# A weight block's load split by head pairs: one transfer of 128 rows or four of 32

## The chip, the cores and the metric

The kernel runs on one core of a Trainium2 chip. The metric is the device time of one execution in microseconds (us), the median of several. The engines go by their short names: PE is TensorE (matrix products), PEld its weight loads, DVE is VectorE, ACT is ScalarE, POOL is GpSimd, and SP is SyncE, which here issues nearly all DMA transfers. The transfers themselves are carried by the core's 16 DMA engines.

## What is computed

Two layers, one after the other. The first is an mLSTM cell over 4 batches, 8 heads, 768 steps and a head width of 40. The second is a feed-forward layer whose activation is h·cos(h). Between them the heads are laid side by side, so that a row of x holds 8 x 40 = 320 numbers.

```python
# q, k, v, o_gate: (4, 8, 768, 40) float32;  i_gate, f_gate: (4, 8, 768)
for t in range(S):
    m_new = np.maximum(f_gate[:, :, t] + m, i_gate[:, :, t])
    f_stab, i_stab = np.exp(f_gate[:, :, t] + m - m_new), np.exp(i_gate[:, :, t] - m_new)
    m = m_new
    C = f_stab[..., None, None] * C + i_stab[..., None, None] * np.einsum('bhd,bhe->bhde', vt, kt)
    n = f_stab[..., None] * n + i_stab[..., None] * kt
    y[:, :, t] = sigmoid(o_gate[:, :, t]) * (C @ qt) / max(|n . qt|, 1)
x = y.transpose(0, 2, 1, 3).reshape(3072, 320)
h = x @ w_in            # w_in: (320, 2048)
out = (h * np.cos(h)) @ w_out   # w_out: (2048, 320)
```

The two weights reach the device as 64-bit floating-point numbers, because the inputs are made that way. The kernel loads their 32-bit halves and makes float32 of them on the chip.

## The kernel before

The sequence is cut in 6 chunks of 128 steps (`c`), and each chunk has 4 batches (`b`). A pair is a cell, with the number n = 4c + b. The kernel first runs the four cells of chunk 0 (`first_cells`). Then, for every chunk c and every b, it runs `both_parts(c, b)`: a quarter of the feed-forward layer of chunk c, beside the cell (c+1, b) of the next chunk. The instructions of each engine are laid out by hand (a manual schedule) and are carried out in this order.

w_in is loaded in four blocks of 512 columns, `weights_in(0)` to `weights_in(3)`, each used by one b of the first chunk. A row of x is split: the first 32 of every head's 40 numbers go into two operands of 128 rows (four heads each: head 2k+i of pair k goes to operand i), and the remaining 8 of the eight heads into a third of 64 rows. The rows of w_in are brought into the same order by the load. So a block consists of two big pieces and one of leftovers:

```python
WP, WQ = 512, 2 * DM
w_in_bits, w_out_bits = (w.bitcast(I32).rearrange("r (n two) -> r n two", two=2) for w in (moe_w_in, moe_w_out))

def bits_in(n, src, pool, width):
    bits = pool.tile([128, width, 2], I32, name="bits", tag="bits")
    for rows, piece in src:
        nc.sync.dma_start(out=bits[rows, 0:n], in_=piece)
    return bits

def weights_in(f):
    for i in range(NK):                 # NK = 2 big pieces
        src = w_in_bits.rearrange("(k i d) n two -> i k d n two", i=2, d=D)[i, :, 0:DA, ts(f, WP)]
        yield w_in_sb[:, i, ts(f, WP)], bits_in(WP, [(slice(0, 128), src)], pb, WP)
    # ... and the leftovers: two transfers of 64 rows, 8 heads x 8 each
```

Here D = 40 and DA = 32. `src` of a big piece has the dimensions 4 (pairs k), 32 (rows d), 512 columns and 2 words. The pool `pb` has 5 buffers.

A piece that has landed is converted. ACT makes two arrays of its halves, DVE shifts and joins, POOL adds:

```python
def parts(dst, bits):
    ...
    nc.scalar.activation(out=t.bitcast(FP), in_=hi.bitcast(FP), func=AF.Abs)        # L140
    nc.scalar.activation(out=m, in_=lo, func=AF.Copy, scale=2.0 ** -29)             # L142
    return dst, hi, t, m

def join(dst, hi, t, m):
    nc.vector.tensor_scalar(...)            # L146
    nc.vector.tensor_scalar(...)            # L148
    nc.vector.scalar_tensor_tensor(...)     # L150, the last to read the bits
    nc.gpsimd.tensor_tensor(out=dst.bitcast(I32), in0=t, in1=m, op=OP.add)          # L151
```

w_out comes in eight pieces of 640 KB with 128 rows each (`weights_out(p)`, three buffers), which are converted in the same way.

The order of the loads on SP and of the work, cut to what lies around these pieces:

```python
def first_cells():
    ...                         # gates, q, k, v of cells 0 to 2
    load(3)                     # q, k, v of cell 3
    pieces.extend(weights_in(0))
    ...
    load(B)                     # q, k, v of cell 4
    ...
    load_E(B); load_o(1); load_E(B + 1)
    outs.append((0, weights_out(0)))
    ...
    values(2); decay(3); weigh_k(3); state(1); normalize(2); scores(3)
    pg = gates_turn(); warm(1); seam(2); weigh(3)
    join(*parts(*pieces.pop(0)))
    pieces.extend(weights_in(1))
    load(B + 1)
    outs.extend((p, weights_out(p)) for p in range(1, 3))
    seam_out(2); state(2); gates_keep(*pg)
    values(3); normalize(3)
    turn(B)                     # PE turns q and k of cell 4: the first to want them
    join(*parts(*pieces.pop(0)))
    warm(3); seam(3)
    decay_exponents(B)          # DVE, then a mask on POOL; E(4) has to be there
    load_E(B + 2); seam_out(3)
    join(*parts(*pieces.pop(0)))
    state(3); turn_out(B, False); decay(B); weigh_k(B); sigmoid(1)

def both_parts(c, b):
    n = (c + 1) * B + b
    f2 = 2 * b
    up = Up(c, f2)              # PE: x @ w_in, two 128-column blocks (L612, leftovers L615)
    scores(n)
    for e in range(2): up.near(e)      # ACT (L620)
    ...
    for e in range(2): up.rest(e)      # DVE (L623)
    ...
    for e in range(2):
        up.sin(e)                      # ACT (L628)
        up.gate(e)                     # DVE (L632)
    ...
    if begin:                          # c == b == 0
        h = out_parts(); w = parts(*pieces.pop(0))
    elif pieces:
        join(*parts(*pieces.pop(0)))
    ...                                # decay of the next cell (ACT)
    down(c, f2 - 1)                    # PE: @ w_out (L644)
    load(n + 2); values(n); normalize(n); out_join(...); load_E(n + 3)
    ...                                # two more pieces likewise
    up = Up(c, f2 + 1); seam(n); ...; down(c, f2)
    if c == 0 and b + 2 < B:
        pieces.extend(weights_in(b + 2))
    turn(n + 1); ...
```

Of the kernel before, what the change touches and what calls it, by code (L numbers as in the profile page):

```python
# [29 lines left out]
def kernel(  # L30
# [26 lines left out]
    HP = H // 2  # L57
# [9 lines left out]
    DA, DL, T4 = 32, 8, 4  # L67
# [11 lines left out]
    pb = ctx.enter_context(tc.tile_pool(name="pb", bufs=5))  # L79
# [39 lines left out]
    w_in_sb = wp.tile([128, NK, DFF], FP, name="w_in_sb")  # L119
# [5 lines left out]
# [8 lines that stand above are left out]
# [24 lines left out]

    def weights_in(f):
        for i in range(NK):
            src = w_in_bits.rearrange("(k i d) n two -> i k d n two", i=2, d=D)[i, :, 0:DA, ts(f, WP)]  # L160
            yield w_in_sb[:, i, ts(f, WP)], bits_in(WP, [(slice(0, 128), src)], pb, WP)
        src = w_in_bits.rearrange("(h d) n two -> h d n two", d=D)[:, DA:D]

        yield (w_in_l[:, ts(f, 2)].rearrange("p a n -> p (a n)"),
               bits_in(256, [(slice(64 * e, 64 * e + 64), src[:, :, ts(2 * f + e, 256)]) for e in range(2)], pb, WP))
# [492 lines left out]
    def first_cells():  # L658
# [29 lines left out]
        load_o(0, (2, 3))  # L688
        load(3)
        pieces.extend(weights_in(0))  # L690
        wall_in(1, 0, psum_o())
        wall_in(1, 1, psum_o())
# [53 lines left out]
        weigh(3)  # L746
# [4 lines that stand above are left out]
# [35 lines left out]
    def both_parts(c, b):  # L786
# [94 lines left out]
        if c == 0:  # L881
            if b + 2 < B:
                pieces.extend(weights_in(b + 2))
            h = out_parts()
# [45 lines left out]
```

## Time and profile before

| | |
|---|---|
| median of 3 runs | 575.06 us (574.02 to 575.40) |
| span of the profiled execution | 572.1 us |
| PE busy | 547.9 us, 96% |
| DVE, ACT, POOL busy | 350.7, 262.6, 84.7 us |
| moved by DMA | 56.79 MB, 99 GB/s over the span |
| w_in's big transfers | 8 of 512 KB |
| w_in's leftovers | 8 of 128 KB |
| w_out's transfers | 8 of 640 KB |

The page of the profile has the busy time of each engine, then the span cut in 40 equal slices, with a digit for the busy share of each slice in tenths (9 is 90% or more). PEclk is the clock that PE was granted, in the same tenths. The DMA share of a window is the mean busy share of the 16 DMA engines; it can come out above 1 where packets overlap. The chain that ended last is followed back from the last instruction, at each step to what released it. A row of waits reads: engine and instruction that waited, the one it waited for, us in total, how often, the longest. In a row of a window come the window, its length, for each engine its busy us and number of instructions, then PE's clock, the DMA share and GB/s. L612 is a line of the kernel.

### The profile page before, as it was taken

To read this page: it belongs to the slowest core of one execution; us is meant where nothing else is said; L and a number is where in the kernel's file an instruction comes from. 1 tells how busy PE (TensorE), PEld (TensorE's weight loads), DVE (VectorE), ACT (ScalarE), POOL (GpSimd) and SP (SyncE) were. 2 spreads that over 40 slices of the span, in tenths; PEclk is the share of its full clock that TensorE was granted. 3 is DMA by queue.
4 is the path that set the end of the run, shared out by engine and by line. 5 is a ranking of instruction groups with operands and counts; after the bars stand their busy time and mean duration, and the time that the engine had idled before them with its cause. 6 is when DMAs were issued, how large, how long until landed. Compare 5 with 4: busy or idle time off the path is not lost.

```text
span 572.1 us, 8809 instructions
## 1 busy us (share of the span) xinstructions
PE 547.9 (96%) x3247; PEld 326.9 (57%) x3247; DVE 350.7 (61%) x690; ACT 262.6 (46%) x418; POOL 84.7 (15%) x114
## 2 busy tenths in 40 slices
PE   8969894999999999999999999999999999999997
PEld 6855462666566556555565565566555555545554
DVE  5756746675777676676676676676676675313221
ACT  4837728577464255264255264255264341323222
POOL 5522413342311011011011011010000000000000
PEclk9979996999999999999999999999999999999999
DMA  9846695576026564226655026665026200010001
GB/s 140 189 127 181 192 205 155 152 181 144 12 77 135 121 134 103 58 87 135 141 127 127 14 82 131 134 138 131 15 87 144 47 15 1 16 45 1 0 0 46
DMA packets 134026, 56.79 MB, mean 99 GB/s; under 512 B 71600, under 2 KB 130048, under 8 KB 133984
## 3 DMA queue, kind: packets, MB, share of 16 engines
q1 hardware_dynamic: 133840, 56.04, 42.6%
q8 instruction: 25, 0.41, 0.3%
q0 software_dynamic: 96, 0.18, 0.1%
q14 instruction: 17, 0.14, 0.1%
q10 hardware_dynamic: 48, 0.02, 0.0%
HBM read 50.00 MB, written 6.21 MB: 98 GB/s over the span
## 4 chain that ended last, share of the span: by engine, by line
PE 82%; DMA 8%; SPq 4%; DVE 2%; ACT 2%; issue 1%; POOL 1%; ACTq 0%; POOLq 0%
PE po L644 36%; PE pup L612 27%; PE pup L615 8%; DMA bits<-in_moe_w_in_dram 5%; PE hp L482 3%; PE ps L439 3%; DMA qs<-in_q_dram 3%; PE pu L579 2%; SPq L321 2%; PE hp L476 2%; SPq L292 1%; PE pt L420 1%; PE ph L464 1%; POOL w_out_sb L151 1%; ACT wt L140 0%
## 5 line engine op out<-in xcount | busy, mean ns | idle before, releaser
L644 PE MATMUL po<-w_out_sb,g 128*128 128x320 f32 x768 | 220.5, 441 | 4.9 <-POOL w_out_sb L151 4.9
L644 PEld LDWEIGHTS po<-w_out_sb,g 128*128 128x128 f32 x768 | 143.4, 192 | 71.1 <-issue 9.7
L612 PE MATMUL pup<-xT,w_in_sb 128*128 128x512 f32 x384 | 175.0, 598 | 2.0 <-POOL w_in_sb L151 1.7
L620 ACT ACTIVATE n<-pup 128x512 int32<-128x512 f32 x96 | 51.9, 592 | 216.6 <-PE pup L615 216.6
L623 DVE SCALAR_TENSOR_TENSOR n<-pup,n 128x512 f32<-128x512 f32 x96 | 61.8, 685 | 143.6 <-ACT n L620 143.6
L612 PEld LDWEIGHTS pup<-xT,w_in_sb 128*128 128x128 f32 x384 | 71.0, 190 | 78.3 <-issue 67.2
L628 ACT ACTIVATE n<-n 128x512 f32<-128x512 f32 x96 | 58.7, 630 | 11.6 <-DVE n L623 11.6
L365 POOL TENSOR_SCALAR_AFFINE_SELECT E<-E 128x1024 f32<-128x1024 f32 x19 | 20.7, 1091 | 290.5 <-DVE E L364 251.9
L632 DVE SCALAR_TENSOR_TENSOR g<-pup,n 128x512 f32<-128x512 f32 x96 | 61.6, 683 | 1.7
L615 PE MATMUL pup<-xT,w_in_l 64*128 64x512 f32 x192 | 54.2, 641 | 0.3 <-POOL w_in_l L151 0.3
L615 PEld LDWEIGHTS pup<-xT,w_in_l 64*128 64x128 f32 x192 | 14.5, 185 | 36.8 <-issue 34.9
L445 DVE TENSOR_TENSOR E<-ps,E 128x512 f32<-128x512 f32 x48 | 30.6, 679 | 3.4 <-PE ps L439 3.4
L404 DVE STREAM_TRANSPOSE t<-qs 128x512 f32<-128x512 f32 x32 | 32.3, 1088 | 0.0
L373 ACT ACTIVATE E<-E 128x1024 f32<-128x1024 f32 x21 | 22.2, 1057 | 21.5 <-POOL E L365 16.8
L439 PEld LDWEIGHTS ps<-t,t 40*128 40x128 f32 (+1 forms) x384 | 25.0, 188 | 9.7 <-issue 9.2
L439 PE MATMUL ps<-t,t 40*128 40x128 f32 (+1 forms) x384 | 25.8, 274 | 0.0
L364 DVE TENSOR_TENSOR E<-E,tab 128x1024 f32<-128x1024 f32 x19 | 23.1, 1213 | 4.0 <-DMA E<-M_d 4.0
L140 ACT ACTIVATE wt<-bits 128x512 f32<-128x512 f32 (+2 forms) x20 | 13.4, 668 | 26.3 <-DMA bits<-in_moe_w_in_dram 19.8
L373 ACT ACT_TABLE_LOAD x18 | 23.1, 1283 | 0.3
L775 ACT ACT_TABLE_LOAD x18 | 23.1, 1283 | 0.3
L579 PEld LDWEIGHTS pu<-vs,kw 128*104 128x104 f32 x160 | 17.0, 177 | 9.8 <-issue 9.8
L496 DVE STREAM_TRANSPOSE room<-hp 128x128 f32<-128x128 f32 x32 | 8.5, 305 | 22.5 <-PE hp L482 22.5
(130 smaller groups left out, 455.4 us busy)
## 6 DMA issues: line engine op xcount, KB each, us to landing
E<-M_d SPq DMA_DIRECT2D x22, 512.0 KB
bits<-in_moe_w_out_dram SPq DMA_DIRECT2D x8, 640.0 KB
bits<-in_moe_w_in_dram SPq DMA_DIRECT2D x8, 512.0 KB
room<-G_d SPq DMA_DIRECT2D x32, 128.0 KB
ks<-in_k_dram SPq DMA_DIRECT2D x24, 160.0 KB
vs<-in_v_dram SPq DMA_DIRECT2D x24, 160.0 KB
out_dram<-o_sb SPq DMA_DIRECT2D x24, 160.0 KB
qs<-in_q_dram SPq DMA_DIRECT2D x32, 80.0 KB
```

What stands on the lines that cost most here:

```text
L373: nc.scalar.activation(out=Es[n], in_=Es[n], func=AF.Exp, scale=-1.0)
L404: nc.vector.transpose(out=dst.rearrange("r p (t x) -> r p x t", x=T4), in_=src.rearrange("r p (x d) -> r p x d", x=T4)[:, :, :, 0:32])
L439: nc.tensor.matmul(ps[j][:, p], kT[r, p], qT[r, p], start=True, stop=True)
L445: nc.vector.tensor_tensor(out=w, in0=pss[n][j], in1=w, op=OP.mult)
L579: nc.tensor.matmul(pu[0:PR, p].rearrange("p j d -> p (j d)"), pair(kws[n], p)[:, 0:PR], vs[n % NB][:, 2 * p:2 * p + 2].rearrange("p j d -> ...
L612: nc.tensor.matmul(pu, w_in_sb[:, i, ts(block(f2, e), 128)], x(i), start=(i == 0), stop=False)
L615: nc.tensor.matmul(pu, w_in_l[r, f2], x(NK, r), start=False, stop=True)
L620: nc.scalar.activation(out=self.n[e], in_=self.pu[e], func=AF.Copy, bias=0.25)
L623: nc.vector.scalar_tensor_tensor(out=self.n[e].bitcast(FP), in0=self.pu[e], scalar=0.25, in1=self.n[e], op0=OP.add, op1=OP.subtract)
L628: nc.scalar.activation(out=r, in_=r, func=AF.Sin, scale=TWO_PI_DOWN)
L632: nc.vector.scalar_tensor_tensor(out=g, in0=self.pu[e], scalar=TWO_PI, in1=self.n[e].bitcast(FP), op0=OP.mult, op1=OP.mult)
L644: nc.tensor.matmul(po[c][b], gs[c, f][:, ts(b, C)], w_out_sb[:, f], start=(f == 0), stop=(f == NF - 1))
```

## The change

The source of a big piece is no longer handed over as one access pattern of 4 groups of 32 rows. Each head pair gets a transfer of its own: 32 rows of 4096 bytes, into its own 32 partitions of the same buffer. The transfers go out one after the other on SP, where the one stood. What is loaded, where to, and everything after it stay as they are. It is meant to make the loading of w_in's pieces better suited to the DMA engines.

```diff
     def weights_in(f):
         for i in range(NK):
+
             src = w_in_bits.rearrange("(k i d) n two -> i k d n two", i=2, d=D)[i, :, 0:DA, ts(f, WP)]
-            yield w_in_sb[:, i, ts(f, WP)], bits_in(WP, [(slice(0, 128), src)], pb, WP)
+            yield w_in_sb[:, i, ts(f, WP)], bits_in(WP, [(ts(h, DA), src[h]) for h in range(HP)], pb, WP)
         src = w_in_bits.rearrange("(h d) n two -> h d n two", d=D)[:, DA:D]
```

HP is 4, so `h` counts head pairs here. The empty line that is added shifts all later lines of the kernel by one: L612 of the kernel before is L613 of the changed one.

## The prediction

> **What bounds the kernel now.** I read the page first: the busy row and the slices, then the chain that ended last, then the waits of TensorE (PE) and ScalarE (ACT), then windows.
>
> ```profile
> PE 547.9 (96%) x3247; PEld 326.9 (57%) x3247; DVE 350.7 (61%) x690; ACT 262.6 (46%) x418; POOL 84.7 (15%) x114
> PE   8969894999999999999999999999999999999997
> PEclk9979996999999999999999999999999999999999
> PE 82%; DMA 8%; SPq 4%; DVE 2%; ACT 2%; issue 1%; POOL 1%; ACTq 0%; POOLq 0%
> ```
>
> PE is the bound, but not everywhere. A slice is 572.1/40 = 14.3 us; from the eighth on (100 us) PE shows 9 in every slice but the last, at full clock. The holes are in slices 1, 3, 5 and 7, and 3 and 7 have a lower clock too. So whatever is gained is gained before about 104 us, and whatever arrives earlier at 104 us ends earlier at 572, because after it PE has nothing to wait for. The 8% of DMA in the chain are two transfers of w_in of 12.09 and 13.83 us (at 46.02 and 73.90 in the chain by time), and one of q of 15.96 us (at 23.64).
>
> The waits of PE from 20.95 to 104.73 us, then ACT's from 20 to 155 (us in total, times, longest):
>
> ```profile
> PE px L568 <- DVE z L536: 5.8, 1, 5.8
> PE pt L420 <- DMA qs<-in_q_dram: 5.5, 1, 5.5
> PE po L644 <- POOL w_out_sb L151: 4.0, 3, 2.3
> PE pup L612 <- POOL w_in_sb L151: 1.7, 1, 1.7
> ...
> ACT wt L140 <- DMA bits<-in_moe_w_in_dram: 19.8, 4, 11.6
> ```
>
> The first two rows are one story. At 81 us ACT, which works in order, stands 11.64 us at the conversion of a w_in piece (released at 87.81); VectorE (DVE) behind it stands 10.61 us; its z comes late and PE waits 5.8 us. The second: the q of cell 4 was issued at 23.64, right behind w_in's first pieces, and landed at 39.61, while PE was ready at 34.2.
>
> Why are those transfers slow? Windows, with the columns PEclk, DMA share and GB/s at the end. The first lies inside the transfer of the w_in pieces issued at 20.95, the other six are the kernel's stages:
>
> ```profile
> 31.00:39.00 8.00, 3.22 (x30) 2.79 (x28) 3.96 (x11) 3.98 (x10) 1.26 (x1) 0.85 0.24 82
> ...
> 20.95:44.55 23.60, 18.07 (x160) 15.46 (x160) 12.93 (x33) 12.28 (x24) 6.72 (x6) 0.86 0.56 127
> 44.55:66.93 22.38, 20.95 (x107) 12.94 (x107) 16.07 (x31) 19.09 (x29) 7.95 (x9) 1.00 0.59 155
> 66.93:104.73 37.80, 27.09 (x118) 17.24 (x116) 23.49 (x44) 19.02 (x37) 12.08 (x12) 0.86 0.77 198
> 104.73:128.56 23.83, 23.83 (x118) 15.40 (x117) 16.03 (x34) 16.83 (x33) 8.63 (x9) 1.00 0.68 170
> 128.56:152.27 23.71, 22.83 (x108) 14.42 (x108) 16.52 (x30) 16.34 (x28) 6.93 (x7) 1.00 0.44 96
> 152.27:173.70 21.43, 21.43 (x145) 12.49 (x145) 15.62 (x33) 9.81 (x16) 3.63 (x3) 1.00 0.24 66
> ```
>
> In 31 to 39 us the share of 16 engines is 0.24: four busy, twelve idle. The stage of c=0, b=1 lasts 37.80 us; its neighbours, with much the same matmuls, last 23.83 and 23.71.
>
> **What the Trainium skill says.** "DMA: Bandwidth & Descriptors", section on why a DMA increments its semaphore by 16: an HWDGE transfer runs on k engines, the largest k up to 16 that divides the slowest dimension of both access patterns. The source of a big w_in piece is 4 head pairs x 32 rows x columns against 128 partitions: k = 4. The trace agrees: each of these eight transfers has 5 semaphore updates at landing (4 engines, and the sequencer for the rest), the transfers of w_out, q, k, v have 16, and so have the gates' 32-row transfers. The same page, rules for kernel authors, says not to split a transfer over partition halves, because each half already uses all 16 engines; here that premise fails. "TensorE: Matmul & The Clock Gate", Part 1: PE's clock is gated down after idleness and let up again by sustained work. The trace agrees: half clock from 36.7 to 43.5 and from 91.3 to 101.5 us, each after one of the two idles, and nowhere else between 6 us and the end.
>
> **The change, part by part.**
>
> *Adds.* Eight 512 KB transfers become 32 of 128 KB: 24 more issues on SP. The trace's uncontended 16-engine issues take 0.40 (32 gate rows) to 0.57 us, the k=4 ones 0.54 to 0.71. Eight at 0.47 with their gap, less two at 0.67: about +2.4 us of SP for each of the four stages. A piece now has four semaphores to be waited for instead of one; not a tenth of a microsecond. The order of instructions on PE, DVE, ACT and POOL is unchanged.
>
> *Takes away.* Two big pieces now take four engines 64 rows of 4096 B each; at 165 (median) to 210 ns (mean) a row that is 10.6 to 13.4 us, with leftovers and queue 16 to 18 us until the second has landed (20.95 to 37.88; 73.90 to 92.81). With 32 rows over 16 engines it is 2 rows a transfer and engine, 16 for both pieces: 2.6 to 3.4 us. As a check, 640 KB of w_out on 16 engines landed in 4.5 to 6.7 us from issue.
>
> *Moves, step 1 (up to 44.55 us).* w_in's first pieces issue at 20.95 to 24.8, land by about 27, the leftover by 28.5. q of cell 4 issues at 26.1 and lands near 29.5 (1024 rows of 160 B, 64 an engine, 14 to 18 ns each, 1.1 us a transfer), E(4) near 33.5 instead of 44.23. PE goes on at 34.2 instead of 39.74: 5.5 us. The half clock there goes too. Behind it the work of DVE and POOL decides: DVE ends z(3) at 36.4, joins piece 1 until 38.0, subtracts for E(4) until 39.2, the mask on POOL ends 40.4, then ACT runs exp, table load and sigmoid until 44.0, before it evacuates the first up matmul. In the trace that starts at 50.30: about **6.3 us** gained.
>
> *Step 2 (b=0, 22.38 us).* It ends in PE waiting 1.70 us for w_in_sb. ACT's 2.99 us of waiting for a piece at 58.19 goes, so DVE's gate ends 2 us earlier and the joins too: **1.7 us**. At b=1's start PE waits 0.98 us for w_out_sb; that chain moves by about 2.2, so **0.5** more.
>
> *Step 3 (b=1, 37.80 us).* w_in's third block is issued behind w_out's piece 3, which waits for one of three buffers, free at about 54 us; it lands by 64; ACT wants it at 68. The 11.6 us wait goes, and PE's 5.8 and 2.26 us of idle, and the half clock (10.2 us, with some 7 us of matmul in it, 3 to 3.5 us). The stage then is its matmuls: up 4.6 + scores 0.9 + down 4.5 + pq 0.9 + values 1.8 + up 4.6 + seam 1.6 + down 4.5 + turn 0.9 = 24.3, with a first wait of 0.4 to 0.8 left, 25. Of 37.8 less the 2.2 of step 2, 35.6, that is **10.6 us**.
>
> *Step 4 (b=2 on).* PE is busy 23.83 of 23.83; w_in's last block lands about 88 against a need at 93. **0.** At b=3 a wait of 0.88 us for w_out_sb stays.
>
> Sum: 6.3 + 2.2 + 10.6 = 19.1 us. Some of these chains I only followed by hand, and a chain not seen now may end last; I take off 0.6. 575.06 - 18.5 = 556.5.
>
> **Rivals.**
> 1. *SP takes the place.* SP stays in order, only eight transfers are in flight (each waits for the one eight before it), and ten issues stand where four stood. If each took 1 us or more, q, k and E behind them would land late. For it: issues of 3 to 9.7 us stand in the trace. Against: these stand behind the four full engines (the 9.66 us of v at 29.25 ends as w_in lands), so the change removes their cause. It would leave perhaps half: 565.
> 2. *The conversion becomes the bound.* Each piece costs ACT 1.3, DVE 1.6, POOL 1.3 us. In b=1 DVE shows 23.49 us of work, close to the 25 that I give the stage. Against: some 5 us of that are b=0's joins, which lag, and b=2 runs PE without a hole with 16.03. If it holds, step 3 gives 7 instead of 10.6: 560.
> 3. *DMA is full, whatever the engines.* The share is 1.10 in the first 21 us and 0.77 in b=1; squeezing b=1 into 25 us makes it 1.1, if nothing is spread differently. But w_in then is a third of what it was in any one engine, and much of b=1's traffic may lie earlier. If loads then end late, 562.
> 4. *More than I say:* if sigmoid and exp in step 1 overlap better, or the b=3 wait goes too, 554.
>
> **Range and chances.** The two idles of PE with their clocks are the solid part: 5.5 + 5.8 + 2.3 + 1.7 + 3 = 18.3 us without any chain by hand, so even two thirds of it is over 2% (11.5 us). The range of 552.5 to 562 holds rivals 2 to 4. Rival 1 alone puts it at 2% or less. Faster by over 2%: 0.94, within: 0.05, slower: 0.01.
>
> **What would show it.** Right: 16 landings for each w_in transfer; no 0.24 stretch; ACT's wait for w_in bits under 2 us; q's wait of PE gone; full clock from 6 us to the end; b=1 of about 25 us; everything from b=2 on with the same lengths, about 19 us earlier. Wrong: SP issues of w_in over 1 us each with PE waiting for qs or E; or waits for w_out_sb grown to several us in b=1 with DVE full; or a DMA share near 1 from 45 to 85 us with ACT still waiting for bits.

## The result and the profile after

The changed kernel takes 555.10 us (four runs, 555.07 to 555.99) against 574.74 us before (574.02 to 575.40): a ratio of 0.9662, with a 95% interval of 0.9645 to 0.9679. It is 19.6 us faster; 556.5 had been predicted. The span of the profiled execution went from 572.1 to 553.4 us.

DMA's slices on the page of the kernel before:

```profile
DMA  9846695576026564226655026665026200010001
```

The page of the changed kernel (busy row, PE's slices, PE's clock, DMA's slices, the chain by engine):

```profile
PE 542.2 (98%) x3247; PEld 322.9 (58%) x3247; DVE 351.0 (63%) x690; ACT 262.8 (47%) x418; POOL 85.8 (16%) x114
...
PE   8998999999999999999999999999999999999997
...
PEclk9999999999999999999999999999999999999999
DMA  9999969560265751166634065635065000000001
...
PE 90%; DVE 5%; POOL 2%; issue 1%; ACT 1%; DMA 0%; POOLq 0%; ACTq 0%; DVEq 0%
```

The deep holes of PE are gone, the clock is full all the way, and the chain holds no DMA any more: 8% became 0%. The first five slices of DMA are all 9, where some were 4 to 6.

The waits of the changed kernel: PE's over the span, and ACT's from 20 to 140 us (us in total, times, longest):

```profile
PE po L645 <- POOL w_out_sb L151: 2.7, 3, 1.0
...
PE pup L616 <- POOL w_in_l L151: 0.9, 1, 0.9
PE pup L613 <- POOL w_in_sb L151: 0.5, 1, 0.5
...
ACT wt L140 <- DMA bits<-in_moe_w_in_dram: 1.0, 1, 1.0
```

PE's waits of 5.8 us for z and 5.5 us for q are no longer there, and ACT's 19.8 us of waiting for w_in are 1.0 us, all at one place. What is left of PE's waits in these stages is for conversions (POOL), but for 0.3 us for DVE's g; none is for a transfer.

Windows of the changed kernel, one for each stage, with PEclk, DMA share and GB/s at the end:

```profile
20.95:37.26 16.31, 16.31 (x160) 14.17 (x159) 12.10 (x33) 12.31 (x24) 5.47 (x5) 1.00 1.03 194
37.26:60.99 23.73, 21.21 (x107) 12.86 (x107) 19.33 (x35) 19.75 (x30) 11.05 (x10) 1.00 1.04 237
60.99:85.97 24.98, 24.00 (x117) 15.14 (x116) 19.67 (x38) 18.39 (x35) 10.58 (x10) 1.00 0.81 210
85.97:109.64 23.67, 23.67 (x118) 15.24 (x117) 17.56 (x36) 16.88 (x34) 9.46 (x10) 1.00 0.76 169
109.64:133.35 23.71, 22.82 (x109) 14.40 (x108) 16.48 (x31) 16.44 (x29) 6.93 (x7) 1.00 0.44 94
```

The start and b=0 together end at 60.99 instead of 66.93, 5.94 us earlier. The stage b=1 is 24.98 us long instead of 37.80: 12.82. The stages b=2 and b=3 have their old lengths, 23.67 and 23.71 from first up matmul to first up matmul (the window of 23.83 us shown for b=2 before ends 0.16 us inside b=3). 5.94 + 12.82 = 18.76, and the spans differ by 18.7: everything was gained before 86 us.

### The profile page after: what moved, and what is told of

Same layout as the page of the kernel before. It is cut to its first block, busy times and chain, and to the rows that moved or that the text cites. A ratio compares the mean times of both kernels' runs of the same rounds, so it can differ in the third digit from the quotient of the medians.

```text
span 553.4 us, 8844 instructions
## 1 busy us (share of the span) xinstructions
PE 542.2 (98%) x3247; PEld 322.9 (58%) x3247; DVE 351.0 (63%) x690; ACT 262.8 (47%) x418; POOL 85.8 (16%) x114
## 4 chain that ended last, share of the span: by engine, by line
PE 90%; DVE 5%; POOL 2%; issue 1%; ACT 1%; DMA 0%; POOLq 0%; ACTq 0%; DVEq 0%
PE po L645 38%; PE pup L613 29%; PE pup L616 9%; PE ps L440 4%; PE hp L483 3%; PE pu L580 3%; PE ph L465 2%; PE hp L477 2%; DVE wt L146 1%; PE pt L421 1%; DVE wt L150 1%; DVE wt L148 1%; POOL w_out_sb L151 1%; PE pq L455 0%; DVE n L624 0%
## 5 line engine op out<-in xcount | busy, mean ns | idle before, releaser
L613 PE MATMUL pup<-xT,w_in_sb 128*128 128x512 f32 x384 | 175.2, 598 | 0.8 <-POOL w_in_sb L151 0.5
L613 PEld LDWEIGHTS pup<-xT,w_in_sb 128*128 128x128 f32 x384 | 70.8, 190 | 77.5 <-issue 66.5
L629 ACT ACTIVATE n<-n 128x512 f32<-128x512 f32 x96 | 58.8, 630 | 11.6 <-DVE n L624 11.6
L387 POOL TENSOR_TENSOR kw<-ks,tab 128x512 f32<-128x512 f32 x20 | 20.9, 1043 | 0.1
```

The lines of the kernel that those rows point to most:

```text
L613: nc.tensor.matmul(pu, w_in_sb[:, i, ts(block(f2, e), 128)], x(i), start=(i == 0), stop=False)
L629: nc.scalar.activation(out=r, in_=r, func=AF.Sin, scale=TWO_PI_DOWN)
```

## The experiments

**Which blocks bring it.** First one block at a time is split, the other three keep the old transfer. The edit for block 0; the others differ by the number:

```diff
-            ... bits_in(WP, [(ts(h, DA), src[h]) for h in range(HP)], pb, WP)
+            ... bits_in(WP, [(ts(h, DA), src[h]) for h in range(HP)] if f == 0 else [(slice(0, 128), src)], pb, WP)
```

Block 0: 

> Only w_in's first block is split by head pairs; blocks 1 to 3 keep one transfer for each big piece. Theory (the four engines of a k=4 transfer were the bottleneck, and each block's gain is its own stage's): the gain of the first stage alone, about 6 us, so 568.5 to 569.5; PE's wait for q of cell 4 gone, half clock only near 90 us. Rival (the gain is of one piece and comes from SP or from the queue as a whole): no gain without the other blocks, 574 to 575.

Block 1: 

> Only the second block is split. Theory: ACT's 3 us of waiting for the first piece of this block and PE's 1.7 us of waiting for w_in_sb go, so 572.5 to 573.5. Rival: 574 to 575, as the 1.7 us are lost again in the stage b=1, which stands 11.6 us at the third block anyway. That stage waits for the DMA of block 3, which is issued at the same time unless SP also gets there earlier, so this rival is a real one.

Block 2: 

> Only the third block is split. Theory: the stage c=0, b=1 shrinks by some 11 us (37.8 to about 27 less what block 1 gave): 563 to 565; no ACT wait for this block, half clock only near 37 to 43 us. Rival (whole queue): under 5 us gained, over 570.

Block 3: 

> Only the last block is split. Theory: nobody waited for it, so the same time as before, 574.5 to 575.5, although its transfers land in 6 us instead of 18. Rival (a queue freed from four full engines helps the later loads): 1 us or more gained. The four single gains together should give the 19.6 us of the whole change, if the blocks don't help each other.

| split | us | before, same chip | ratio (95%) |
|---|---|---|---|
| block 0 | 567.92 | 574.37 | 0.9884 (0.9847 to 0.9922) |
| block 1 | 567.57 | 574.37 | 0.9879 (0.9852 to 0.9906) |
| block 2 | 569.99 | 574.37 | 0.9925 (0.9903 to 0.9948) |
| block 3 | 574.24 | 574.37 | 0.9996 (0.9982 to 1.0009) |

Block 3 came out as the theory had it, with no gain, though its two pieces landed 10.2 us after their issue (96.76 to 106.99) where 6 had been expected. Block 0 brought 6.45 us where about 6 had been expected; its time lies 0.6 us below the expected range, which is within its interval of plus or minus 2.2. Blocks 1 and 2 did not follow it: block 1, for which PE had waited only 1.7 us, brought 6.8 us, and block 2, at which ACT stood for 11.6 us, only 4.4. So the idea that each block's gain goes by the waits that end at its own landing fell. The four single gains add up to 17.8 us and not to 19.6, which is within their intervals.

The traces say why. Those of blocks 0, 1 and 2 come from the quickest execution of each kernel (565.26, 566.01 and 567.90 us), so they show where the time goes and not the size of the median gain. Part of the spread lies ahead of b=0: in the five traces that are alike up to there, with block 0 unsplit, this stage began at 43.17 to 45.40 us. Below are SP's issues of block 2 and the first conversion of it on ACT, with block 1 alone split, then with block 2 alone split (start us, length us, what; the idle time before it and its releaser in brackets):

```profile
66.82 4.03 SPq L131 DMA_DIRECT2D bits<-in_moe_w_in_dram  x4
...
80.71 0.67 ACT L140 ACTIVATE wt<-bits 128x512 f32<-128x512 f32 x1 [7.29 <-DMA bits<-in_moe_w_in_dram]
```

```profile
73.99 4.26 SPq L131 DMA_DIRECT2D bits<-in_moe_w_in_dram  x7
...
82.59 0.67 ACT L140 ACTIVATE wt<-bits 128x512 f32<-128x512 f32 x1 [6.04 <-DMA bits<-in_moe_w_in_dram]
```

With block 1 split, block 2 is issued 7 us earlier and still takes 13.8 us to land. With block 2 split, it is issued as late as before, but its first piece lands after 8.5 us. ACT's 11.64 us of waiting for this piece became 7.29 and 6.04, so each cures about half. What block 1 did to SP stands in SP's own timeline around the load of k for cell 5, before and then after:

```profile
51.41 9.43 SPq L321 DMA_DIRECT2D ks<-in_k_dram  x1
```

```profile
47.31 0.84 SPq L322 DMA_DIRECT2D ks<-in_k_dram  x1
```

Behind the unsplit block this single issue held SP for 9.43 us, and SP works in order, so that everything behind it, block 2 included, was issued late. In the other traces with block 1 in one transfer a piece on four engines (block 0, 2 or 3 alone, and the run with a busy PE below) this issue lasted 9.7 to 10.6 us; in all with block 1 split by head pairs 0.5 to 0.9.

The stage b=1 in the traces, from its first up matmul to that of b=2, with block 2's issue counted from its start and ACT's wait for block 2's first piece (us):

| split | stage b=1 | block 2 issued at | ACT's wait |
|---|---|---|---|
| none | 37.80 | +7.0 | 11.64 |
| block 0 | 35.48 | +5.9 | 11.35 |
| block 1 | 31.30 | +1.0 | 7.29 |
| block 2 | 31.95 | +6.8 | 6.04 |
| blocks 0 and 1 | 31.23 | +0.5 | 7.06 |
| blocks 1 and 2 | 25.92 | +0.3 | 2.12 |
| all | 24.98 | -0.8 | 0.95 |

From the single blocks came a new theory: a slow block costs twice, by its own landing and by holding back SP for the next. Two runs with two blocks split were to test it by the times.

Blocks 0 and 1: 

> Blocks 0 and 1 are split, 2 and 3 are not. New theory (a slow block costs twice: by its own landing and by holding back SP, so that the next block is issued later): block 2 is issued near 60 us as in the changed kernel, its first piece lands some 13.5 us later, near 73.5, ACT wants it at 68.5, so it waits about 5 us, of which some 2.3 us are hidden because PE comes to the seam only then: 557.5 to 559. Rival (each block's gain is its own, so the single gains of 6.5 and 6.8 us add): 561.

Blocks 1 and 2: 

> Blocks 1 and 2 are split, 0 and 3 are not. New theory: block 2 is issued near 66.8 us as with block 1 alone, its first piece lands 8.5 us later, near 75.3, ACT wants it at 73.3; 2 us of waiting are hidden by PE's slack, so all of the loss in b=1 is gone and only block 0's 6 us are left: 561 to 562. Rival (the single gains of 6.8 and 4.4 us add): 563.2.

Blocks 0 and 1 gave 560.75 us (before 574.50; ratio 0.9757, 0.9725 to 0.9790), blocks 1 and 2 gave 560.96 (0.9768, 0.9738 to 0.9798). The second is the new theory's number (to 0.04 us) and better than the sum of the single gains. The first is the sum's number and misses the new theory's range by 1.8 us: block 2 was issued at 61.51 and its first piece was there at 75.5, ACT waited 7.1 us for it (5 were expected), and one wait of PE for w_out_sb grew to 3.2 us. With intervals of plus or minus 1.3 to 2.1 us on the single gains, the times do not decide between the two.

The stage b=1 says more. Block 1 alone took 6.50 us off it, though PE had waited only 1.70 us for block 1 itself; what it adds is block 2's earlier issue, by which ACT's wait fell by 4.35 us. So the double cost is seen there. That two splits help each other beyond this is not: blocks 1 and 2 together took 11.88 us off the stage, alone 6.50 and 5.85, and beside block 1 block 0 took nothing more off it (31.23 against 31.30). Each row is one execution.

**Is it the number of engines, or just smaller transfers?** Four transfers for each piece again, but cut by columns, so that each still has four groups of rows:

```diff
-            ... [(ts(h, DA), src[h]) for h in range(HP)] ...
+            for h in range(4):
+                nc.sync.dma_start(out=bits[:, ts(h, WP // 4)], in_=src[:, :, ts(h, WP // 4)])
```

> Each big piece goes in four transfers, as in the changed kernel, but cut by columns: 4 groups x 32 rows x 1 KB each. Same number of issues and bytes, slowest dimension 4. Theory (engine count): four engines as before, 5 updates at each landing, a DMA share near 0.25 beside them, so no gain: 573 to 578. Rival (smaller transfers, more of them in flight, are what helps): 555 to 560.

And two transfers of two head pairs each:

```diff
-            ... [(ts(h, DA), src[h]) for h in range(HP)] ...
+            ... [(ts(h, 2 * DA), src[ts(h, 2)]) for h in range(2)] ...
```

> Each big piece goes in two transfers of 2 groups x 32 rows. Theory: the slowest dimension is 2, so two engines carry 128 rows a piece each, 21 to 27 us a piece and 42 to 54 us a block; blocks 0 and 2 hold up the loads behind them by some 25 us more each and block 1 too: 625 to 670, DMA share near 0.12 in the stretches. Rival (any split is better than none): under 575.

The cut by columns took 571.39 us against 574.73 (ratio 0.9950, 0.9929 to 0.9971): 3.3 us gained, not none, and not 19.6. Its transfers show 5 semaphore updates, as before: one soon after the issue (1.0 to 1.3 us in the kernel before) and 4 at landing. Those of the two pairs show one early and 2 at landing, those of the changed kernel 16 at landing. So, read as in the prediction, the engines are 4, 2 and 16. In the column cut block 0 as a whole landed at 36.59 us, hardly before the 37.88 of the kernel before, since four engines had the same bytes to carry; but its first piece was complete at 29.69 instead of 32.26, and block 2's at 84.4 instead of 87.7. In the traces 2.3 of the 2.9 us between the spans (572.1 and 569.2) are won in the stage b=1, which waits for block 2 and lasts 35.54 us.

Two pairs took 611.68 us (ratio 1.0632, 1.0599 to 1.0666). A split that lowers the engine count from 4 to 2 loses 37 us, which decides against "any split helps". The waits of ACT in that run, from 20 to 200 us:

```profile
ACT wt L140 <- DMA bits<-in_moe_w_in_dram: 54.0, 8, 14.4
```

The 19.8 us became 54.0. My estimate of 625 to 670 was too high by a slip of counting: a piece has 128 rows, so two engines carry 64 each, not 128. The landings came mostly 5.0 to 5.8 us apart for 256 KB.

**What the 24 more issues on SP cost.** One transfer a piece again, but of 128 rows that follow each other; the kernel leaves out the reordering of the rows and so uses other weights, with the same work:

```diff
-            ... [(ts(h, DA), src[h]) for h in range(HP)] ...
+            ... [(slice(0, 128), w_in_bits[ts(i, 128), ts(f, WP)])] ...
```

> Each big piece is one transfer again, of 128 rows that follow each other in w_in (rows 0 to 127 and 128 to 255) instead of the head pairs' rows: the kernel leaves out the reordering of the rows, so it multiplies by other weights than the reference; the work is the same. Theory: 16 engines with one issue each, 24 issues less than the changed kernel: 554 to 555.5, the extra issues being beside other work. Rival (SP's 24 issues cost something on the path): 552 to 553.5. Rival (the four separate landings matter): 560 or more.

555.12 us (ratio 0.9657, 0.9635 to 0.9680), the changed kernel's time to two hundredths: the issues cost nothing, and four separate landings are of no use as such. Here ACT doesn't wait for block 2 at all, and yet nothing is gained, so the last 1.0 us of that wait in the changed kernel was hidden too.

**Other transfers on four engines.** In the later chunks, x's transposed halves are written to DRAM with the same 4 x 32 pattern. Split as well, on top of the change:

```diff
         for i in range(2):
-            nc.sync.dma_start(out=xd[:, i], in_=xl[:, i])
+            for h in range(HP):
+                nc.sync.dma_start(out=xd[h, i], in_=xl[ts(h, DA), i])
```

> The changed kernel, with the other k=4 transfers split too: the write of x's transposed halves to DRAM (4 groups x 32 rows x 512 B, 32 of 64 KB) becomes 128 transfers of 32 rows, in the later chunks. Theory: a transfer on few engines costs only where somebody waits for it; PE has no idle time there, so 554.5 to 556. Rival (the loads behind these writes, or SP's 96 more issues, tell): over 0.4% either way.

555.69 us (ratio 0.9666, 0.9643 to 0.9690): the same. (In the trace the stage b=1, which lies ahead of these writes, is 0.7 us longer than in the changed kernel's, and that is the difference of the spans.) SP's waits for these writes to land, for the changed kernel and then for this one:

```profile
SPq L516 <- DMA X_d<-room: 49.6, 23, 4.4
```

```profile
SPq L517 <- DMA X_d<-room: 17.6, 19, 2.5
```

32 us of SP's waiting vanished without a trace in the time. From the first up matmul of b=2 to the end it is 467.4 us in both.

**How much of it was the clock?** The kernel before, with PE kept busy in its two idles by products of zeros:

```diff
         normalize(3)
+        warm(24)
         turn(B)
...
         up = Up(c, f2 + 1)
+        if c == 0 and b == 1:
+            for _ in range(40):
+                nc.tensor.matmul(po[c][0], nil, nil[:, 0:1].to_broadcast([128, DM]), start=False, stop=False)
```

> The kernel before, with PE given products of zeros in its two long idles: 24 of 512 columns before it turns q and k of cell 4, and 40 of 320 columns, added as zeros to an open sum, ahead of the seam of cell 5. The waits for q and w_in stay. Theory (part of the loss was the half clock after the idles, some 1.5 us at 37 to 43 and 3 to 3.5 us at 91 to 101): 570 to 571.5, full clock throughout. Rival (the clock cost nothing because DVE and ACT set the pace behind the idles): 574 to 575.

574.44 us against 574.47 (ratio 0.9990, 0.9975 to 1.0006): no gain, the rival was right. From the first idle to 44.55 us, where the up matmuls of the kernel before start, and from the second idle to those of b=2, the kernel before and then this one; last, a wait of PE in this one:

```profile
34.21:44.55 10.34, 4.81 (x26) 3.52 (x26) 3.96 (x11) 2.87 (x9) 2.52 (x2) 0.67 0.56 133
87.18:104.73 17.55, 9.52 (x36) 7.17 (x36) 13.51 (x28) 13.77 (x27) 7.89 (x8) 0.71 0.53 156
```

```profile
34.12:44.55 10.43, 10.00 (x55) 5.36 (x55) 3.75 (x11) 4.18 (x13) 2.54 (x2) 1.00 0.57 136
87.74:105.42 17.68, 13.89 (x77) 9.82 (x76) 13.21 (x28) 13.76 (x27) 7.86 (x8) 0.90 0.54 154
...
PE pup L615 <- POOL w_in_l L151: 1.8, 1, 1.8
```

The clock rose from 0.67 to 1.00 and from 0.71 to 0.90. Behind the first idle the up matmuls started at 43.11 instead of 44.55, but then waited 1.80 us for w_in_l instead of 0.33, and the stage b=1 began at 67.46 instead of 66.93. The second window kept its length, 17.68 against 17.55. Its matmuls ended sooner and then waited 3.26 us for w_out_sb instead of 2.26: the late conversions set the pace. Half clock of 3.4 us remained in the second window, so it isn't excluded that a clock kept full there would have shown something; that was not tried.

**An attempt to go further.** The changed kernel, with the second piece's conversion ahead of the seam of cell 2:

```diff
         outs.extend((p, weights_out(p)) for p in range(1, 3))
+        join(*parts(*pieces.pop(0)))
         seam_out(2)
...
         turn(B)
-        join(*parts(*pieces.pop(0)))
```

> The changed kernel, with the conversion of w_in's second piece moved ahead of cell 2's seam_out on ACT and of cell 3's normalize on DVE, into a gap of 1.45 us that DVE has there since the piece lands at 28.3 us. Theory (the start is now bounded by the chain of conversions): the up matmul's waits of 0.46 and 0.94 us go and exp and sigmoid move up, 553.3 to 554.3. Rival (the seam behind it is delayed by the 1.3 us on ACT and eats it): 555 to 556.

554.98 us (554.77 to 555.49) against the changed kernel's 555.10: no difference that these runs can show, and not the 553.3 to 554.3 of the theory. PE's waits of 0.5 and 0.9 us for the conversions are gone, but a new one stands for them, for z, which now comes behind the conversion on DVE:

```profile
PE px L569 <- DVE z L537: 1.3, 1, 1.3
```

No version here beats the changed kernel by more than its spread.

## Why the prediction was right, point by point

*The bound and the place.* Right: two idles of PE before 104 us, both from w_in's transfers on few engines, and a PE-bound rest that passes the gain on unchanged. The engine count is shown by the landings and by the runs with 4, 2 and 16 engines.

*Adds.* An issue took 0.42 us mostly, 0.31 to 0.87 in all, and with its gap 0.46 where SP ran free, for 0.47 assumed. Its cost on the path is nothing, as the single-transfer run shows.

*Takes away.* Mis-sized. For both pieces 2.6 to 3.4 us were worked out; in block 0 the eight transfers landed from 25.03 to 28.97, 0.56 us apart, so about 4.5 us for eight. The term that failed is a row's time: 165 to 210 ns were carried over from the old transfers, but with 2 rows an engine in 0.56 us a row took 280 ns. The number of engines is not the reason. By the median, a packet of 4096 bytes took 159 to 165 ns in the blocks of the kernel before, on four engines, 159 ns in the single 128-row transfers on sixteen, and 260 to 281 ns in the changed kernel's transfers of 32 rows; why these are slower is not shown. It did no harm, as nobody waited that closely. The check beside this term ("640 KB of w_out on 16 engines landed in 4.5 to 6.7 us from issue") holds for six of the eight transfers; the two issued behind slow blocks at 78.52 and 105.74 landed after 17.2 and 13.2 us, which was a sign of what a slow block does to the loads behind it.

*Step 1.* 6.3 us predicted to ACT's first evacuation; it went from 50.30 to 44.27, 6.0. By the start of b=1, 5.94 were left. PE went on after values(3) without a wait for q, though q landed at 31.65 and E(4) at 35.97, some 2 us later than worked out.

*Step 2.* The 1.7 us came: at the scores behind the first up block of b=1 (73.39 before, 65.75 after) the gain is 7.64 us instead of 5.94. The further 0.5 us did not: the wait for w_out_sb at the start of b=1 is 0.98 us as before.

*Step 3.* The total is right, its parts are not. Stage b=1 lost 12.82 us, where 1.7 + 0.5 + 10.6 = 12.8 had been predicted, and 24.98 us is its new length, where 25 had been. But block 2 was said to be issued at 54 and landed by 64; it was issued at 60.17, its first piece landed at 69.30, and ACT waited 0.95 us. The missing 6 us were lost on SP. Between the seventh and the eighth issue of block 1 (41.68 and 44.83) it waited for w_out's first piece to land, because only eight transfers are in flight, and the issues of q, k and v for cell 6 took 1.21, 3.55 and 1.66 us (this k takes 3.1 to 3.9 us in every trace, whatever is split). So w_out's piece 3 went out at 58.41, 4.4 us after its buffer was free. The delay cost nothing because PE reached the seam at 79.46, 2.3 us after z was ready. And the 3 to 3.5 us put down to the half clock were no term of their own: keeping most of the clock up, with the waits in place, gained nothing. The sum was safe since the stage was built from its matmuls at full clock, not from the old length less single savings. The list under "solid part", 18.3 us, which added the clock to the idles, came out near the truth by luck.

*Step 4.* Right: 23.67 and 23.71 us, and the wait of 0.9 us at b=3 stays.

*Rivals.* SP as the new bound did not come. Full conversions did not either: PE shows 24.00 of 24.98 us in b=1, with DVE at 19.67. The full DMA came as a fact, with shares of 1.03, 1.04 and 0.81 where 0.56, 0.59 and 0.77 stood, but without its consequence. (The prediction's own working gives 0.77 x 37.8 / 25 = 1.16 for b=1, not 1.1; it measured 0.81.)

*Not foreseen.* That block 1 was worth 6.8 us, because it held back SP, while block 2 alone brought only 4.4 us (the intervals of the two overlap). The prediction went by the waits that end at a block's own landing, and the expectations for the single blocks, made in the same way, were off by 5 to 6 us for block 1 and by 5 to 7 for block 2. For all blocks at once this did not show, since the stage b=1 was built from its matmuls.

## What to carry to other kernels

Look at how many semaphore updates a load has when it lands: if it is 5 and not 16, the source's outermost dimension keeps it on four engines, and handing each group over as its own transfer of 32 rows cost only issues here. Look then for who waits; the same cure on the writes of x's halves took 32 us from SP's waits and nothing from the time. And ask of a slow transfer not only who waits for its data, but also what its queue makes late: what block 1 made late cost about as much as the slow landing of block 2 (the stage b=1 lost 6.5 us with block 1 alone split, 5.9 with block 2 alone).

## What the runs showed of the hardware

- In transfers of 32 rows the rate went up 2.5 times with 4 times the engines. 512 KB on four engines landed 5.1 to 6.3 us apart (58.11 and 63.84 in block 1: 5.7), which is 23 GB/s an engine; 256 KB on two mostly 5.3 us apart, 25 GB/s an engine; 128 KB on sixteen 0.56 us apart in block 0, 15 GB/s an engine and 234 GB/s in all, with SP's issues 0.46 us apart. A single 512 KB transfer of 128 rows on sixteen landed 1.98, 1.92, 1.45 and 1.35 us after the one before it in the four blocks; 1.98 us is 265 GB/s.
- An issue can hold SP for long: the same k took 9.4 to 10.6 us to issue behind a block of two 512 KB transfers on four engines, and 0.5 to 0.9 behind the same block split over sixteen.
- The DMA share is no count of engines. It read 0.24 in the stretch that I took for "four busy, twelve idle", 0.55 in a like stretch of the column cut (33 to 36 us), w_in also on four engines (0.28 of the 0.55 is 160-byte rows of other loads), and 0.28 with two (33 to 46 us). The number of landings is the safe reading.
- Part of PE's half clock can be free. 6.8 us of it at the first idle and 6.8 of 10.2 us at the second were taken away, and the time stayed the same, because PE only waited longer for the next conversion.
